# Conversion of w_k split between TensorE and GpSimd, VectorE's start in a written order, and fewer, larger loads

## The chip, the cores and the metric

The kernel runs on one core of a Trainium2 chip. The metric is the device time of one execution in microseconds (us); the median of several runs is compared.

## The reference

Three stages follow each other, for 8 batches of 576 positions. Linear attention with an RMS norm gives `x`; a gated two-layer network with a one-position shift turns it into a second `x`; a causal attention of four experts (two chosen per position) gives the output. The first two stages, in which all of the change lies:

```python
kv  = np.einsum('bhsd,bhse->bhde', k, v)             # 8 heads of 64
out = np.einsum('bhsd,bhde->bhse', q, kv)
x   = out / np.sqrt(np.mean(out * out, -1, keepdims=True) + 1e-6) * g_norm
...
xk = mu_k * x + (1.0 - mu_k) * x_prev                # x_prev: x one position earlier
xr = mu_r * x + (1.0 - mu_r) * x_prev
k  = np.maximum(xk @ w_k, 0.0)                       # 512 x 1024
v  = k * k @ w_v                                     # 1024 x 512
r  = 1.0 / (1.0 + np.exp(-(xr @ w_r)))               # 512 x 512
return r * v
```

## The kernel before

Every large product runs as three fp32r matmuls: an operand is split into a high and a low half, and high by high, high by low and low by high are added in PSUM (`mm3`, lines 75 to 79). A batch's 576 positions are cut into two halves (h) of 288.

Phase A goes through the batches. Its **front** (`Front`) forms kv from five chunks of k and v (`chunk`, L294), multiplies by q (`heads`, L311), forms mean squares (`means`, L323), takes their inverse root on VectorE in a chain of steps that each need the one before (`rsqrt`, L329 to L338), spreads it over the partitions with TensorE (`spread`, L345) and scales x (`scaled`, L351). A **mix** (`mix`) makes the inputs `xr` or `xk` of one half: for each of four 128-row pieces ScalarE scales the shifted x, VectorE adds the other part (`xm`, L402), ScalarE rounds it to the high half `mixh`, VectorE subtracts for the low half `mixl` (L397). An **r group** is 12 matmuls with w_r and a sigmoid, a **k group** 12 matmuls with w_k, a Relu on ScalarE and a square on GpSimd (`ksq`). Batch 0 has 8 r groups and 16 k groups.

The weights w_r, w_k and w_v come as 64-bit floats. `converted` turns a 128 by 512 chunk of w_r (chunks 0 to 3) or w_k (4 to 11) into halves: ScalarE takes the absolute value of the upper word, VectorE builds an fp32 number `t` from it in three steps (L213, L215, L217), ScalarE rounds it to the high half, VectorE makes the part that the lower word adds in two steps (L204, L206). TensorE then adds `t`, minus the high half and minus that part in PSUM (L249 to L251), and ScalarE writes the sum out as the low half. There are three buffers for `t` (`cvt`). `value_blocks` converts w_v likewise during batches 1 to 6, with an addition on GpSimd (L468) in the place of TensorE's sum, one buffer `vraw` for the loaded words, and one step per `run(vals)`.

**What sets the order.** The tile framework's scheduler orders each engine's instructions by its own estimate of time. Instructions issued through `vec`, `act` and `ten` (class `InOrder`) while their `on` is set keep their written order among themselves; others are put between them. Before, all three are on until the r groups of batch 0's first half are written, and then off. Loads and stores go through the queues of SyncE and ScalarE; in the built program each transfer takes the next of eight semaphores in rotation, and is issued only when the semaphore's previous transfer has landed.

At the end of the conversions for w_r VectorE has the means' chain of batch 0, two mixes for w_r, then the mixes for w_k and the conversions that are left; TensorE can start r groups when the first mix is there, and k groups when chunks 4 to 7 and the first mix for w_k are there.

Of the kernel before, what the change touches and what calls it, by code (L numbers as in the profile page):

```python
# [25 lines left out]
def tile_kernel(ctx: ExitStack, tc: tile.TileContext, qT, k, v, g2, mu_k, mu_r, w_r, w_k, w_v, w_qk, w_vg, w_o, out):  # L26
    nc = tc.nc
    P = 128
    B, S, DM = k.shape
# [23 lines left out]
    g_sb = const.tile([P, 1], F32, name="g_sb")  # L53
    muk = const.tile([P, KD], F32, name="muk")
    mur = const.tile([P, KD], F32, name="mur")
    nuk = const.tile([P, KD], F32, name="nuk")
    nur = const.tile([P, KD], F32, name="nur")
# [124 lines left out]
    def phase_a():  # L182
        W["vb"] = ExitStack()
        vb = W["vb"].enter_context(tc.tile_pool(name="vb", bufs=1, side="right", reuse_waits="tile"))
        with ExitStack():
# [71 lines left out]
            def load_kv(i, eng=nc.sync):  # L257
                b, c = divmod(i, NF)
                if b < B and i not in kvt:
# [4 lines left out]
                    kvt[i] = (kt, vt)  # L264

            def load_q(i, eng=nc.sync):
                b, c = divmod(i, 4)
                if b < B and i not in qts:
                    qt = fr.tile([P, 2, HS], F32, name="qt", bufs=4)
                    eng.dma_start(qt, qT[b, c])  # L270
                    qts[i] = qt
# [3 lines left out]
            class Front:  # L275
# [10 lines left out]
                def chunk(self, c):  # L286
                    t0, n = FH[c]
                    kt, vt = kvt[self.b * NF + c]
                    for a in range(NP):

                        for r in range(2):
                            hd = 2 * (2 * (a // 2) + r) + a % 2
                            hd = slice(hd * D, (hd + 1) * D)
                            ten.matmul(self.kw[r * D:(r + 1) * D, a, :], kt[:n, hd], vt[:n, hd],  # L294
                                       start=(c == 0 and a == 0), stop=(c == NF - 1), skip_group_check=True)
                    load_kv((self.b + 1) * NF + c)
# [7 lines left out]
                def heads(self, h, a):  # L304
                    i = 4 * self.b + 2 * h + a
                    qt = qts[i]
                    po = pf.tile([P, 2, 512], F32, name="po", bufs=2)
                    for c in range(2):
                        for r in range(2):
                            rs = slice(r * D, (r + 1) * D)  # L310
                            ten.matmul(po[c * D:(c + 1) * D, r, :HS], self.kv[rs, 2 * a + c, :], qt[rs, c, :], start=True, stop=True, skip_group_check=True)  # L311
                    load_q(i + 4)
# [123 lines left out]
            def value_blocks():  # L436
# [23 lines left out]
                def value(n):  # L460
                    nonlocal raw
                    t = fr.tile([P, CW], F32, name="cvt", bufs=3)
# [46 lines left out]
            for i in range(4):  # L509
                load_q(i)  # L510
            for i in range(KD, len(wts)):
                wload(i, nc.sync)
            for nu, mu in ((nuk, muk), (nur, mur)):
                vec.tensor_scalar(nu, mu, -1.0, 1.0, op0=ALU.mult, op1=ALU.add)
# [52 lines left out]
            for e in (vec, act, ten):  # L567
                e.on = False
# [41 lines left out]
            for b in range(1, B):  # L610
# [9 lines left out]
                for n, (g, h, m) in enumerate(groups):  # L620
# [10 lines left out]
                    run(f, vals)  # L631
                    if n < 2 * KD:
# [488 lines left out]
```

## Time and profile before

| | |
|---|---|
| median of 3 runs | 1000.81 us (999.16 to 1003.89) |
| profiled execution, its time | 996.78 us |
| its span, first to last instruction | 995.0 us |
| TensorE matmul busy | 955.1 us (96%) |
| VectorE / ScalarE / GpSimd busy | 643.1 / 538.8 / 414.4 us |
| mean granted TensorE clock | 0.991 of full |

The profile of one execution gives, for each instruction, its engine, line, output and inputs, start and length, the idle time of its engine just before, and what ended that idle time. A line of 67 is that of the recording helper, whatever the operation. Matmuls and VectorE instructions overlap at their ends, so the distance between two starts can be shorter than the length of the first. Phase A fills about the first 430 us, the second product (with w_v) follows until about 615 us, then the expert attention.

### The profile page before, as it was taken

How to read it: one execution, taken by the hardware profiler on the slowest of the kernel's cores; microseconds unless marked ns; L12 is line 12 of the kernel's file. 1: busy time of each engine (PE TensorE's matmuls, PEld its weight loads, DVE VectorE, ACT ScalarE, POOL GpSimd, SP SyncE). 2: the span in 40 equal slices, each digit the busy share in tenths (PEclk: the TensorE clock that was granted, in tenths of full speed). 3: DMA queues.
4: the chain of work that ended last, by engine and by line, in shares of the span. 5: the costliest groups of instructions: out<-in, count | busy, mean ns of one | idle time of the engine just before them, and what ended most of it. 6: DMA issues, size and time to landing. Idle time of an engine off the chain costs nothing.

```text
span 995.0 us, 21152 instructions
## 1 busy us (share of the span) xinstructions
PE 955.1 (96%) x7936; PEld 871.4 (88%) x7936; DVE 643.1 (65%) x1532; ACT 538.8 (54%) x1326; POOL 414.4 (42%) x510
## 2 busy tenths in 40 slices
PE   5599999999999999999999999999999999999998
PEld 3478898999999989999899999888989888888986
DVE  4874694856585945549888884566555565656562
ACT  5583756565665756445544442546364546455544
POOL 0013052424251513465878886436162534335231
PEclk9799999999999999999999999999999999999999
DMA  9652737263726313858566652002020202020102
GB/s 328 225 182 80 225 100 224 76 232 112 234 103 214 105 67 98 291 180 250 177 235 196 210 161 100 27 23 84 14 96 2 96 7 90 27 70 27 49 13 84
DMA packets 82742, 127.22 MB, mean 128 GB/s; under 512 B 7632, under 2 KB 58320, under 8 KB 82640
## 3 DMA queue, kind: packets, MB, share of 16 engines
q1 hardware_dynamic: 65744, 104.11, 31.6%
q10 hardware_dynamic: 16896, 21.76, 7.0%
q8 instruction: 63, 1.03, 0.4%
q14 instruction: 39, 0.32, 0.1%
HBM read 78.66 MB, written 47.19 MB: 126 GB/s over the span
## 4 chain that ended last, share of the span: by engine, by line
PE 74%; DVE 8%; DMA 6%; ACT 6%; POOL 3%; issue 2%; SPq 0%; ACTq 0%; DVEq 0%; POOLq 0%
PE acc L77 15%; PE acc L78 14%; PE acc L79 14%; PE qa L671 6%; PE qd L671 4%; PE acc L671 4%; PE pt L940 3%; PE acc L967 3%; DMA x2in<-x2d 3%; PE s L891 3%; ACT pr L903 2%; POOL x2l L777 2%; PE acc L294 2%; POOL pr L920 1%; DMA vt<-in_v 1%
## 5 line engine op out<-in xcount | busy, mean ns | idle before, releaser
L431 POOL TENSOR_TENSOR ksq<-rl 128x288 f32<-128x288 f32 x128 | 97.3, 765 | 162.2 <-ACT rl L429 157.9
L77 PE MATMUL acc<-mixh,wkh 128*128 128x288 f32 x512 | 152.6, 298 | 0.0
L78 PE MATMUL acc<-mixl,wkh 128*128 128x288 f32 x512 | 152.1, 297 | 0.0
L79 PE MATMUL acc<-mixh,wkl 128*128 128x288 f32 x512 | 151.0, 295 | 0.0
L903 ACT ACTIVATE pr<-pr,nm 128x256 f32<-128x256 f32 (+4 forms) x144 | 83.2, 580 | 65.0 <-DVE nm L857 64.8
L920 POOL TENSOR_SCALAR pr<-pr,rc,wg 128x512 f32<-128x512 f32 (+3 forms) x128 | 76.7, 612 | 99.6 <-DVE wg L850 60.8
L77 PEld LDWEIGHTS acc<-mixh,wkh 128*128 128x128 f32 x512 | 96.0, 187 | 1.9 <-issue 1.1
L79 PEld LDWEIGHTS acc<-mixh,wkl 128*128 128x128 f32 x512 | 96.4, 188 | 0.7 <-issue 0.4
L78 PEld LDWEIGHTS acc<-mixl,wkh 128*128 128x128 f32 x512 | 96.1, 188 | 0.9
L683 POOL TENSOR_TENSOR sgv<-ct,sgv 128x288 f32<-128x288 f32 x64 | 81.3, 1294 | 36.6 <-DVE ct L681 36.0
L429 ACT ACTIVATE rl<-acc 128x288 f32<-128x288 f32 x128 | 51.9, 407 | 76.9 <-PE acc L79 64.5
L397 DVE TENSOR_TENSOR mixl<-xm,mixh 128x288 fp32r<-128x288 f32 x120 | 59.8, 530 | 50.1 <-ACT mixh L403 49.6
L857 DVE CUSTOM_DVE_ANT_0 pr<-s,mask 128x256 f32<-128x256 f32 (+4 forms) x144 | 66.9, 482 | 18.8 <-PE pt L940 11.8
L77 PE MATMUL acc<-mixh,wrh 128*128 128x288 f32 x240 | 73.9, 308 | 0.5 <-ACT sg L67 0.5
L77 PE MATMUL acc<-x2h,wqh 128*128 128x320 f32 (+1 forms) x240 | 74.3, 310 | 0.0
L79 PE MATMUL acc<-mixh,wrl 128*128 128x288 f32 x240 | 72.1, 300 | 0.0
L78 PE MATMUL acc<-mixl,wrh 128*128 128x288 f32 x240 | 72.0, 300 | 0.0
L79 PE MATMUL acc<-x2h,wql 128*128 128x320 f32 (+1 forms) x240 | 71.1, 296 | 0.0
L78 PE MATMUL acc<-x2l,wqh 128*128 128x320 f32 (+1 forms) x240 | 70.9, 295 | 0.0
L73 DVE TENSOR_TENSOR kk<-tv,kk 128x1152 fp32r<-128x1152 f32 x32 | 58.7, 1852 | 8.4 <-ACT kk L72 8.4
L940 PE MATMUL pt<-ident,pr 128*128 128x128 f32 x400 | 62.6, 276 | 1.1 <-ACT pt L949 0.5
L72 ACT ACTIVATE kk<-tv 128x1152 fp32r<-128x1152 f32 x32 | 37.3, 1167 | 38.5 <-POOL tv L160 15.6
(236 smaller groups left out, 2788.0 us busy)
## 6 DMA issues: line engine op xcount, KB each, us to landing
kkd<-ksq SPq DMA_DIRECT2D x128, 144.0 KB, 1.8
kin<-kkd SPq DMA_DIRECT2D x32, 576.0 KB, 4.9
qt<-in_qT SPq DMA_DIRECT2D x32, 288.0 KB, 4.8
sgv<-sgd SPq DMA_DIRECT2D x16, 576.0 KB, 3.8
x2d<-sgv SPq DMA_DIRECT2D x16, 576.0 KB, 3.2
sgd<-sg ACTq DMA_DIRECT2D x56, 144.0 KB, 3.5
out<-ob SPq DMA_DIRECT2D x28, 288.0 KB, 2.1
kt<-in_k SPq DMA_DIRECT2D x24, 256.0 KB, 4.6
```

What stands on the lines that cost most here:

```text
L73: vec.tensor_sub(lo, src, hi.bitcast(F32))
L77: ten.matmul(ps, wh(i), xh(i), start=(i == 0), stop=False)
L78: ten.matmul(ps, wh(i), xl(i), start=False, stop=False)
L79: ten.matmul(ps, wl(i), xh(i), start=False, stop=(i == n - 1))
L397: vec.tensor_sub(xl[:, p, :], xs[p], xh[:, p, :].bitcast(F32))
L431: nc.gpsimd.tensor_mul(sq, rl, rl)
L671: nc.tensor.matmul(q[:, :HS], a[:, i, ms_], c[:, i, :], start=(start and i == 0 and n == 0), stop=(stop and i == KH - 1 and n == 2), skip_ ...
L683: nc.gpsimd.tensor_mul(g, c, g)
L857: nc.vector.tensor_tensor_reduce(out=pr[:R, k0:k0 + kn], in0=s[:R, :kn], in1=mk, scale=1.0, scalar=lo, op0=ALU.add, op1=ALU.min, accum_out ...
L903: nc.scalar.activation(pr[:, :L], pr[:, :L], AF.Exp, bias=nm, scale=-1.0, accum_out=sms[b, p, j][:, e2:e2 + 1])
L920: nc.gpsimd.tensor_scalar(pr[:, :L], pr[:, :L], rc[:, r:r + 1], wg, op0=ALU.mult, op1=ALU.mult)
L940: nc.tensor.transpose(pt[:, (i - i0) * P:(i - i0 + 1) * P], pr[:, k1 - P:k1], ident)
```

## The change

1. `vec` stays on longer, until the first mix for w_k is written, so that VectorE's steps of the means, the mixes for w_r, the conversions 4 to 7 and that mix keep their written order. Steps of chunks 8 to 11 are still placed by the scheduler.
2. Chunks 6 to 11 (`LATE = 6`) get their low half otherwise: VectorE's lower-word step writes `vd`, of which there is one buffer, GpSimd adds it to `t`, ScalarE rounds the high half from the sum, VectorE subtracts for the low half. The three matmul steps and ScalarE's copy of these six chunks are gone.
3. k and v of a chunk come in one transfer; q comes in two transfers per batch (two buffers) and not in four; `g_norm`, `mu_k` and `mu_r` come in one transfer on ScalarE's queue and not in three on SyncE's, and the two `1 - mu` steps are one.
4. `value` yields twice before it starts, and every eighth group runs one step more of `vals`.

```diff
@@ weights of phase A @@
+    pars = const.tile([P, 1 + 2 * KD], F32, name="pars")
+    nus = const.tile([P, 2 * KD], F32, name="nus")
+    g_sb, muk, mur = pars[:, :1], pars[:, 1:1 + KD], pars[:, 1 + KD:]
+    nuk, nur = nus[:, :KD], nus[:, KD:]
...
-            wts, raws = [], []
+            wts, raws, LATE = [], [], 6
@@ converted @@
                 next(words)
                 yield
                 next(words)
-                act.activation(h, t, AF.Copy)
-                yield
-                for _ in low_word(lo, hi, t.bitcast(I32), l, -2.0 ** -52):
-                    pass
-                yield
-                acc = acc_tile()
-                ten.matmul(acc, ident, t, start=True, stop=False)
-                ten.matmul(acc, idn, h, start=False, stop=False)
-                ten.matmul(acc, idn, l, start=False, stop=True)
-                act.activation(l, acc, AF.Copy)
+                if i < LATE:
...
+                else:
+                    yield
+                    d = conv.tile([P, CW], F32, name="vd")
+                    for _ in low_word(lo, hi, t.bitcast(I32), d, 2.0 ** -52):
+                        pass
+                    nc.gpsimd.tensor_add(t, t, d)
+                    yield
+                    act.activation(h, t, AF.Copy)
+                    vec.tensor_sub(l, t, h.bitcast(F32))
                 yield
@@ loads @@
-                    kt, vt = [fr.tile([P, DM], F32, name=name, bufs=5) for name in ("kt", "vt")]
-                    nc.sync.dma_start(kt[:n], k[b, t0:t0 + n, :])
-                    eng.dma_start(vt[:n], v[b, t0:t0 + n, :])
+                    t = kvt[i] = fr.tile([P, 2, DM], F32, name="kvt", bufs=5)
+                    nc.sync.dma_start(t[:n].rearrange("p u d -> p (u d)"), kv[b, t0:t0 + n, :])
...
-                    qt = fr.tile([P, 2, HS], F32, name="qt", bufs=4)
-                    eng.dma_start(qt, qT[b, c])
+                    qts[i] = fr.tile([P, 2, 2, HS], F32, name="qt", bufs=2)
+                    nc.sync.dma_start(qts[i], qT[b, h])
...
-                    load_q(i + 4)
+                    if a == 1:
+                        load_q(2 * self.b + h + 2)
@@ value @@
                     nonlocal raw
+                    yield
+                    yield
                     t = fr.tile([P, CW], F32, name="cvt", bufs=3)
@@ start of phase A @@
-            for u, src in ((g_sb, g2), (muk, mu_k), (mur, mu_r)):
-                nc.sync.dma_start(u, src)
             for i in range(KD):
                 wload(i, (act, nc.sync)[i % 2])
+                if i == 1:
+                    act.dma_start(pars, par)
...
             for e in (vec, act, ten):
                 e.on = True
+            vec.tensor_scalar(nus, pars[:, 1:], -1.0, 1.0, op0=ALU.mult, op1=ALU.add)
...
             for m in range(KD):
                 r_group(0, 0, m)
-            for e in (vec, act, ten):
-                e.on = False
+            act.on = ten.on = False
...
                 run(mk)
                 if m < 3:
                     f1.chunk(m + 2)
+            vec.on = False
             f1.state()
@@ later batches @@
                     run(f, vals)
+                    if n % 8 == 7:
+                        run(vals)
```

VectorE, at the means' chain of batch 0 (`ms`, `nt`, `y` are its tiles; `cvt_531` and `cvt_558` are chunks 5 and 6 of w_k). Before:

```order
L67 TENSOR_SCALAR y_374<-nt_375 128x144
L213 TENSOR_SCALAR cvt_531<-cvt_531 128x512
L67 TENSOR_TENSOR nt_375<-y_374 128x144
L215 TENSOR_SCALAR cvt_531<-cvt_531 128x512
L213 TENSOR_SCALAR cvt_558<-cvt_558 128x512
L67 TENSOR_TENSOR nt_375<-nt_375,ms_373 128x144
L217 SCALAR_TENSOR_TENSOR cvt_531<-raw_160,cvt_531 128x512
L215 TENSOR_SCALAR cvt_558<-cvt_558 128x512
L67 SCALAR_TENSOR_TENSOR y_374<-nt_375,y_374 128x144
```

Now:

```order
L66 TENSOR_SCALAR ms_339<-acc_322 128x144
L66 TENSOR_SCALAR nt_341<-ms_339 128x144
L66 TENSOR_SCALAR y_340<-nt_341 128x144
L66 TENSOR_TENSOR nt_341<-y_340 128x144
L66 TENSOR_TENSOR nt_341<-nt_341,ms_339 128x144
L66 SCALAR_TENSOR_TENSOR y_340<-nt_341,y_340 128x144
```

The ten steps of these two chunks that stood between the chain's steps stand behind the mixes for w_r now.

VectorE, behind the last low half for w_r (`mixl`). Before, the first mix for w_k (`xm_671`, `mixl_670`) begins even ahead of it (`mixl_444`):

```order
L402 SCALAR_TENSOR_TENSOR xm_671<-xT_307,muk_86,xm_671 128x288
L67 TENSOR_TENSOR mixl_444<-xm_456,mixh_443 128x288
L402 SCALAR_TENSOR_TENSOR xm_673<-xT_307,muk_86,xm_673 128x288
L397 TENSOR_TENSOR mixl_670<-xm_671,mixh_669 128x288
L402 SCALAR_TENSOR_TENSOR xm_689<-xT_307,muk_86,xm_689 128x288
L397 TENSOR_TENSOR mixl_670<-xm_673,mixh_669 128x288
```

Now twelve steps of chunks 4 to 6 come first, then these: the last of chunk 6 (`cvt_524`), four of chunk 8 (`cvt_590`), the new subtraction of chunk 6, and chunk 7 (`cvt_553`); 26 rows stand between the last `mixl` for w_r and the first `xm` for w_k:

```order
L66 SCALAR_TENSOR_TENSOR vd_558<-raw_143 128x512
L212 TENSOR_SCALAR cvt_590<-cvt_590 128x512
L214 TENSOR_SCALAR cvt_590<-cvt_590 128x512
L216 SCALAR_TENSOR_TENSOR cvt_590<-raw_147,cvt_590 128x512
L203 TENSOR_SCALAR raw_147<-cvt_590 128x512
L66 TENSOR_TENSOR wkl_115<-cvt_524,wkh_114 128x512
L66 TENSOR_SCALAR cvt_553<-cvt_553 128x512 x2
```

The conversions that stood in the chain, and those of chunks 6 to 9, have moved ahead of the first mix for w_k, and the second mix stands between steps of chunks 10 and 11.

TensorE, at the first k group. Before, behind the last r group:

```order
L249 MATMUL acc<-cvt,ident 128x512
L250 MATMUL acc<-wkh,idn 128x512
L251 MATMUL acc<-wkl,idn 128x512
L294 MATMUL acc<-vt,kt 64x64 x29
L77 MATMUL acc<-mixh,wkh 128x288
L78 MATMUL acc<-mixl,wkh 128x288
L79 MATMUL acc<-mixh,wkl 128x288
```

Now:

```order
L300 MATMUL acc<-kvt 64x64 x32
L316 MATMUL po<-qt,kv 64x288 x16
L76 MATMUL acc<-mixh,wkh 128x288 x4
L77 MATMUL acc<-mixl,wkh 128x288
L78 MATMUL acc<-mixh,wkl 128x288
```

All of the next batch's `heads` stand ahead of the k groups now, and four k groups are open at once, piece by piece of the mix; the next four are ordered likewise, and the means of batch 1 stand behind those eight.

## Rows read from the trace of the kernel before

**Rows 1.** Busy time by stretch: start:end us, length, busy per engine, PEclk, DMA share, GB/s

```profile
0.00:47.78 47.78, 26.43 (x224) 18.05 (x225) 32.73 (x82) 25.81 (x49) 1.85 (x17) 0.86 0.81 281
47.78:100.18 52.40, 52.40 (x432) 43.52 (x433) 29.64 (x68) 32.63 (x74) 10.60 (x16) 1.00 0.41 131
100.00:430.00 330.00, 326.26 (x2992) 306.15 (x2991) 213.20 (x428) 200.47 (x480) 114.82 (x139) 0.99 0.49 161
```

**Rows 2.** Timeline of TensorE: start us, us, line, what [idle before, releaser]

```profile
33.67 1.13 PE L67 MATMUL po<-rb,selb 32*128 32x144 f32 x8 [8.59 <-DVE rb L67]
...
47.78 0.40 PE L77 MATMUL acc<-mixh,wrh 128*128 128x288 f32 x1 [0.49 <-ACT sg L67]
...
84.23 1.19 PE L323 MATMUL acc<-sq,sels 128*32 128x144 f32 x32
...
100.18 0.29 PE L77 MATMUL acc<-mixh,wrh 128*128 128x288 f32 x1
```

**Rows 3.** Timeline of VectorE: the means' chain of the first batch, same columns

```profile
25.13 0.31 DVE L67 TENSOR_SCALAR ms<-acc 128x144 f32<-128x144 f32 x1 [6.73 <-PE acc L67]
...
26.01 0.43 DVE L213 TENSOR_SCALAR cvt<-cvt 128x512 f32<-128x512 f32 x1
26.35 0.30 DVE L67 TENSOR_TENSOR nt<-y 128x144 f32<-128x144 f32 x1
...
30.93 0.69 DVE L206 SCALAR_TENSOR_TENSOR wkl<-raw 128x512 fp32r<-128x512 uint32 x1
31.53 0.30 DVE L67 SCALAR_TENSOR_TENSOR y<-nt,y 128x144 f32<-128x144 f32 x1
31.86 0.31 DVE L67 TENSOR_TENSOR nt<-y 128x144 f32<-128x144 f32 x1
...
33.16 0.37 DVE L67 SCALAR_TENSOR_TENSOR rb<-rb,lom,y 128x144 fp32r<-128x144 f32 x1
```

**Rows 4.** Timeline of VectorE: the end of the mixes for w_r

```profile
45.79 0.52 DVE L402 SCALAR_TENSOR_TENSOR xm<-xT,muk,xm 128x288 f32<-128x288 f32 x1
46.22 0.45 DVE L67 TENSOR_TENSOR mixl<-xm,mixh 128x288 fp32r<-128x288 f32 x1
```

**Rows 5.** Chain that ended last, in order of time: start us, us, what

```profile
49.38 0.86 PE acc L249 x2
50.24 0.23 PE acc L250
50.47 0.14 PE acc L78
...
50.74 0.24 PE acc L251
```

**Rows 6.** Timeline of VectorE: first and last step of w_r's fourth chunk

```profile
15.60 0.88 DVE L67 TENSOR_SCALAR cvt<-cvt 128x512 f32<-128x512 f32 x2
...
17.71 0.69 DVE L67 SCALAR_TENSOR_TENSOR wrl<-raw 128x512 fp32r<-128x512 uint32 x1
```

**Rows 7.** Timelines of VectorE and GpSimd: an addition for w_v beside the means' chain

```profile
125.05 1.35 DVE L333 TENSOR_TENSOR nt<-y 128x144 f32<-128x144 f32 x1
...
124.94 1.29 POOL L468 TENSOR_TENSOR cvt<-cvt,vd 128x512 f32<-128x512 f32 x1 [7.31 <-DVE vd L206]
```

**Rows 8.** Timelines of VectorE and ScalarE: the start

```profile
6.91 0.17 DVE L514 TENSOR_SCALAR nur<-mur 128x4 f32<-128x4 f32 x1 [1.34 <-DMA mur<-in_mu_r]
...
5.22 0.66 ACT L67 ACTIVATE cvt<-raw 128x512 f32<-128x512 f32 x1 [2.44 <-DMA raw<-in_w_r]
```

**Rows 9.** Timelines of TensorE (two rows) and ScalarE (one): waits in the later batches

```profile
131.34 0.67 PE L345 MATMUL po<-rb,selb 32*128 32x144 f32 x8 [1.45 <-DVE rb L338]
...
164.41 0.71 PE L311 MATMUL po<-qt,kv 64*64 64x288 f32 x8 [1.87 <-ACT xT L315]
...
163.16 0.65 ACT L314 ACTIVATE sq<-po 128x576 f32<-128x576 f32 x1 [4.42 <-DMA vraw<-in_w_v]
```

**Rows 10.** Busy time by stretch: behind TensorE's wait at 164 us

```profile
164.00:170.00 6.00, 5.59 (x35) 4.15 (x36) 2.08 (x5) 5.60 (x14) 0.10 (x1) 0.72 0.96 284
```

More of the change, by code (lines that the diff above doesn't have):

```diff
@@ L25, in tile_kernel @@
 @with_exitstack
-def tile_kernel(ctx: ExitStack, tc: tile.TileContext, qT, k, v, g2, mu_k, mu_r, w_r, w_k, w_v, w_qk, w_vg, w_o, out):
+def tile_kernel(ctx: ExitStack, tc: tile.TileContext, qT, kv, par, w_r, w_k, w_v, w_qk, w_vg, w_o, out):
     nc = tc.nc
     P = 128
-    B, S, DM = k.shape
+    B, S, DM = kv.shape[0], kv.shape[1], kv.shape[2] // 2
     H = 8
@@ L242, in converted @@
                 next(words)
-                act.activation(h, t, AF.Copy)
-                yield
-                for _ in low_word(lo, hi, t.bitcast(I32), l, -2.0 ** -52):
-                    pass
-                yield
-                acc = acc_tile()
-                ten.matmul(acc, ident, t, start=True, stop=False)
-                ten.matmul(acc, idn, h, start=False, stop=False)
-                ten.matmul(acc, idn, l, start=False, stop=True)
-                act.activation(l, acc, AF.Copy)
+                if i < LATE:
+                    act.activation(h, t, AF.Copy)
+                    yield
+                    for _ in low_word(lo, hi, t.bitcast(I32), l, -2.0 ** -52):
+                        pass
+                    yield
+                    acc = acc_tile()
+                    ten.matmul(acc, ident, t, start=True, stop=False)
+                    ten.matmul(acc, idn, h, start=False, stop=False)
+                    ten.matmul(acc, idn, l, start=False, stop=True)
+                    act.activation(l, acc, AF.Copy)
+                else:
+                    yield
+                    d = conv.tile([P, CW], F32, name="vd")
+                    for _ in low_word(lo, hi, t.bitcast(I32), d, 2.0 ** -52):
+                        pass
+                    nc.gpsimd.tensor_add(t, t, d)
+                    yield
+                    act.activation(h, t, AF.Copy)
+                    vec.tensor_sub(l, t, h.bitcast(F32))
@@ L253, in converted, with load_kv @@
                 yield
             kvt, qts = {}, {}
-            def load_kv(i, eng=nc.sync):
+            def load_kv(i):
                 b, c = divmod(i, NF)
-                if b < B and i not in kvt:
+                if b < B:
                     t0, n = FH[c]
-                    kt, vt = [fr.tile([P, DM], F32, name=name, bufs=5) for name in ("kt", "vt")]
-                    nc.sync.dma_start(kt[:n], k[b, t0:t0 + n, :])
-                    eng.dma_start(vt[:n], v[b, t0:t0 + n, :])
-                    kvt[i] = (kt, vt)
@@ L266, in load_q @@
-            def load_q(i, eng=nc.sync):
-                b, c = divmod(i, 4)
-                if b < B and i not in qts:
-                    qt = fr.tile([P, 2, HS], F32, name="qt", bufs=4)
-                    eng.dma_start(qt, qT[b, c])
-                    qts[i] = qt
+                    t = kvt[i] = fr.tile([P, 2, DM], F32, name="kvt", bufs=5)
+                    nc.sync.dma_start(t[:n].rearrange("p u d -> p (u d)"), kv[b, t0:t0 + n, :])
+            def load_q(i):
+                b, h = divmod(i, 2)
+                if b < B:
+                    qts[i] = fr.tile([P, 2, 2, HS], F32, name="qt", bufs=2)
+                    nc.sync.dma_start(qts[i], qT[b, h])
@@ L310, in heads @@
                             rs = slice(r * D, (r + 1) * D)
-                            ten.matmul(po[c * D:(c + 1) * D, r, :HS], self.kv[rs, 2 * a + c, :], qt[rs, c, :], start=True, stop=True, skip_group_check=True)
-                    load_q(i + 4)
+                            ten.matmul(po[c * D:(c + 1) * D, r, :HS], self.kv[rs, 2 * a + c, :], qt[rs, a, c, :], start=True, stop=True, skip_group_check=True)
+                    if a == 1:
+                        load_q(2 * self.b + h + 2)
                     sq = self.sq[h, a] = fr.tile([P, 2, HS], F32, name="sq", bufs=4)
@@ L461, in value @@
                     nonlocal raw
+                    yield
+                    yield
                     t = fr.tile([P, CW], F32, name="cvt", bufs=3)
@@ L501, in phase_a @@
                     wts.append((wkh[:, i, c:c + CW], wkl[:, i, c:c + CW], w_k, i * P, c))
-            for u, src in ((g_sb, g2), (muk, mu_k), (mur, mu_r)):
-                nc.sync.dma_start(u, src)
             for i in range(KD):
                 wload(i, (act, nc.sync)[i % 2])
+                if i == 1:
+                    act.dma_start(pars, par)
             for i in range(NF):
                 load_kv(i)
-            for i in range(4):
+            for i in range(2):
                 load_q(i)
```

24 lines of the change are left out of this document (7 added, 17 removed).

## The prediction

> **What bounds the kernel now.** I read the busy time by stretch first, then TensorE's timeline, then VectorE's at TensorE's waits. From 100 to 430 us TensorE is busy for 326.26 of 330 us; from 47.78 to 100.18 all the time, in the first 47.78 us for 26.43 only [rows 1]. So work that TensorE loses, or a start that comes sooner, counts in full as long as nothing else becomes late. The start is VectorE's: TensorE waits 8.59 us for the inverse root of the means, and the first r group of the second half starts at 47.78; the means of batch 1 come at 84.23, batch 1's first r group at 100.18 [rows 2]. The sum is made on this profiled execution, 996.78 us; the three runs have a median of 1000.81, and I carry the difference over to that.
>
> **The start.** VectorE waits 1.34 us for mur until 6.91, while ScalarE's first absolute value is done at 5.22 + 0.66 = 5.88 [rows 8]. With one parameter load the first step can come up to 1.0 us sooner. Against that, the first tile of k and v is now issued beside w_r's first chunk, which can land later. Between 1.0 us gained and 0.5 lost I take 0.5 gained.
>
> **The means' chain.** It runs from 25.13 to 33.16 + 0.37 = 33.53, 8.40 us, with ten w_k steps in it; steps that follow each other alone are 0.33 to 0.35 us apart (31.53 to 31.86) [rows 3]. Three first steps take 0.88 us (25.13 to 26.01), nine at 0.345 make 3.10, the cast and the last step 0.64: 4.62. Gain 3.78 us. This has one answer, since VectorE does nothing else there.
>
> **The mixes for w_r.** Three steps of chunk 4 leave the stretch between the chain and the first mix: two SCALAR_TENSOR_TENSOR of 0.60 each (30.93 to 31.53) and one TENSOR_SCALAR of 0.34 (26.01 to 26.35) [rows 3], 1.54 together; the xm for w_k ahead of the last mixl leaves too, 0.43 us (45.79 to 46.22) [rows 4]. I count 1.9. So far 0.5 + 3.8 + 1.9 = 6.2 us: the r group of 47.78 starts at 41.6, and VectorE is done with the mixes for w_r at 46.22 + 0.45 - 6.2 = 40.5.
>
> **Six chunks less on TensorE.** One costs 0.86 + 0.23 + 0.24 = 1.33 us (rows of L249, L250, L251) [rows 5]; six make 8.0 us, all in the stretch where TensorE is the bound. ScalarE loses six copies and gains nothing. With these two gains alone batch 1 would begin at 100.18 - 6.2 - 8.0 = 86.0.
>
> **What is late next.** Everything that left the start, and six new subtractions, now stands on VectorE ahead of or between the mixes for w_k. From 40.5 it has: three steps left of chunk 4, 1.8 us (two thirds of a chunk); seven chunks, at 17.71 + 0.60 - 15.60 = 2.7 us in series [rows 6], or 2.2 where two chunks interleave (three steps of 0.34, two of 0.60 [rows 3]): 5.4 for chunks 5 and 6 in series and 5 x 2.45 = 12.3 for the others; six subtractions, for which no row of that size exists before: between 0.45 (a mixl of 288 columns [rows 4]) and 0.80 (0.45 scaled to 512), taken as 0.60, the step of 512 columns in [rows 3], 3.6; eight xm and eight mixl at 0.43, 6.9. Sum 30.0 us: 70.5.
>
> The six additions on GpSimd are the unknown price. The same operation for w_v takes 1.29 us, and the VectorE step that runs beside it takes 1.35 [rows 7] in place of the 0.30 of the same step at 26.35 [rows 3]: 1.05 us lost each, 6.3 in all, if VectorE always has a step to lose, as here it has. Bounds: 0 and 6 x 1.29 = 7.7. I take 6.3, the row that is nearest, and VectorE ends at 76.8; its last mixl is one subtraction earlier, 76.2.
>
> The Trainium skill ("SBUF — State Buffer", "SBUF: two separate sides") says that VectorE and GpSimd share a port pair as an exclusive lock, held for the whole instruction, so that a VectorE step with two SBUF inputs waits until GpSimd's is over. It speaks against moving these sums to GpSimd beside a saturated VectorE; the row of 1.35 agrees with it. By it each addition would cost up to its whole length, 7.7 us in place of 6.3, and batch 1 would begin 1.4 us later.
>
> In TensorE's new order the eight k groups of the first four column blocks come before the means of batch 1, four open at a time, so that behind the last mixl only eight matmuls of 0.14 [rows 5] are left: 76.2 + 1.1 = 77.3. From the means to batch 1's first r group I keep 100.18 - 84.23 = 15.95 [rows 2]: 93.3. TensorE then waits some 7 us in pieces between about 58 and 76. Behind one wait of 1.87 us at 164 its granted clock averaged 0.72 over 6 us [rows 9, 10], a loss of 1.7. So there is a price of the clock here, between 0 and twice that; I take 1.0. Batch 1 begins at 94.3, a gain of 5.9 where 14.2 were taken out.
>
> **The larger loads and w_v's spacing.** The loads lie beside a busy TensorE from 48 us on, so fewer of them are worth nothing by themselves. But a rotation of eight is passed more slowly. At 158.7 us ScalarE has a store to issue whose semaphore's last user is the vraw load eight transfers earlier; it stands for 4.42 us until that load lands, its next work starts at 163.16, and TensorE waits 1.87 us, with the clock loss of 1.7 behind it [rows 9, 10]. With five loads per batch in place of ten between them, and the load placed otherwise, the eighth transfer comes several groups later. I count 3.6 us. The other wait, 1.45 us at 131.34 for rb [rows 9], is in a chain with w_v steps in it; they still stand there, only later in the chain, so I count 0 to 1.45 and take 0. Two more yields per `value` and three more steps per batch move no work: cover is TensorE's own 326 of 330 us; without that cover a late half of w_v would stop the second product, but 150 steps at 27 a batch end as early as 134 at 24 (5.6 batches). Bounds for the whole item: 0 and 5.1. The scheduler also orders the expert attention's first batches a little differently: 1.5 us either way, taken as 0.
>
> **Sum.** 6.2 + 8.0 - (94.3 - 86.0) = 5.9, and 3.6: 9.5 us off 996.78, 987.3 by the profiled execution; from the median 1000.81, **991.3 us**.
>
> **Rivals.**
> - *GpSimd costs VectorE nothing* and the clock stays up. VectorE's last mixl is then at 69.9, TensorE goes through at 69.9 + 1.1 + 15.95 = 87.0, the gain is 13.2 + 3.6, with rb's wait 1.45 more: some 18 us, 983. For it: the steps of one input may run beside an addition. Against it: the row of 1.35.
> - *The wait eats the gain.* The additions cost their full length (1.4 more), the clock loses 3.4 in place of 1.0, and the store's wait comes back at another transfer: 9.5 - 1.4 - 2.4 - 3.6 = 2.1 us, 998.7, no change that can be measured. For it: every number of this stretch sits on one saturated engine, and any transfer of vraw's size can hold the rotation.
> - *Slower.* A late chunk goes around: VectorE's vd, GpSimd's sum, ScalarE's rounding, VectorE's subtraction, with one vd buffer and three cvt buffers, and ScalarE stands behind the four heads of batch 1 there. If a chunk has to wait for that circle, it costs 0.69 (30.93), 1.29, 0.66 (as ScalarE's step at 5.22) and 0.60, about 3.2 us [rows 3, 7, 8], in place of the 1.05 for each of six: 13 us more. To be slower by 5 us the last mixl must come after 76.2 + 9.5 + 5 = 91. The steps of two other chunks between fill the circle in the new order, and that speaks against it: then about 1004.
> - *The order is not held*: not a case by itself, since the new program shows the chain without w_k steps; the unpinned steps of chunks 8 to 11 ahead of the mix are in the sum.
>
> **Chances.** Forecast as summed, 986 to 995: 0.55. GpSimd free or nearly so: 0.17. Wait eats the gain: 0.22. Slower: 0.06. A measurement of this kernel tells 0.5%, 5 us, from no change. A part of the forecast's own spread lies above 995.8: faster 0.71, within 0.5% 0.24, slower 0.05. The range reaches from the full gain of the first rival to most of the second: 983 to 999.
>
> **What would show it.** The means' chain at 4.6 us; TensorE's first r group of the second half near 41.6; no L249 for six chunks; VectorE without idle time from there to about 76, with steps beside the additions over 1 us; TensorE's new waits for mixl between 58 and 77; batch 1's first r group near 94; no wait at the third batch's heads. I am wrong if TensorE has no waits there (VectorE lighter than summed), if batch 1 begins later than 98, or if the gain of the first 100 us is lost again after it.

## The result

| | before | after |
|---|---|---|
| median of 4 runs each, same chip | 1002.18 us (999.16 to 1003.89) | 991.33 us (990.46 to 991.88) |
| ratio | | 0.9906, 95% interval 0.9883 to 0.9929 |
| span of the profiled execution | 995.0 us | 989.9 us |

The time came out where it was predicted, and 1% faster is more than the measurement is uncertain. The forecast started from the 1000.81 us of three runs; with the fourth the median of before is 1002.18, so the gain is 10.85 us where 9.5 was forecast. But the two profiled executions lie only 5.1 us apart, half of what the medians do, and the terms of the sum did not come out as written. Six marks show where the time went. They are read from the traces: **ms** is VectorE's first step of the means' chain, **r** TensorE's first r group of batch 0's second half, **b1** batch 1's first r group, **middle** from there to the first matmul of the second product, **second** that product up to the start of its last matmul, **rest** what follows to the end of the span (these two to within 0.1 us). The second row is a second profile of the unchanged kernel (experiment 1).

| kernel | ms | r | b1 | middle | second | rest | span |
|---|---|---|---|---|---|---|---|
| before | 25.13 | 47.78 | 100.18 | 321.7 | 191.8 | 381.3 | 995.0 |
| before, second profile | 25.24 | 47.89 | 100.27 | 326.0 | 192.1 | 381.4 | 999.8 |
| after | 27.08 | 44.67 | 97.82 | 315.3 | 190.5 | 386.3 | 989.9 |

So b1 comes 2.4 us sooner (5.9 forecast), the middle is 6.4 or 10.7 us shorter (3.6 forecast), and the rest is 5 us longer (0 forecast).

**The start and VectorE's chain, after.** TensorE's timeline, to hold against [rows 2]; columns are start, length, line and what, and the idle time before with its releaser:

```profile
31.83 1.13 PE L66 MATMUL po<-rb,selb 32*128 32x144 f32 x8 [4.80 <-DVE rb L66]
...
44.67 0.40 PE L76 MATMUL acc<-mixh,wrh 128*128 128x288 f32 x1 [0.58 <-ACT sg L66]
...
64.76 1.33 PE L76 MATMUL acc<-mixh,wkh 128*128 128x288 f32 x4 [2.78 <-ACT mixh L409]
...
81.87 1.19 PE L329 MATMUL acc<-sq,sels 128*32 128x144 f32 x32
...
97.82 0.29 PE L76 MATMUL acc<-mixh,wrh 128*128 128x288 f32 x1
```

VectorE's timeline, to hold against [rows 3, 8]: the wait for the parameters, and the chain:

```profile
7.74 0.17 DVE L66 TENSOR_SCALAR nus<-pars 128x8 f32<-128x8 f32 x1 [5.20 <-DMA pars<-in_par]
...
27.08 0.31 DVE L66 TENSOR_SCALAR ms<-acc 128x144 f32<-128x144 f32 x1 [6.92 <-PE acc L66]
...
31.31 0.37 DVE L66 SCALAR_TENSOR_TENSOR rb<-rb,lom,y 128x144 fp32r<-128x144 f32 x1
```

The chain lasts 31.31 + 0.37 - 27.08 = 4.60 us (before 8.40), and TensorE's wait for it falls from 8.59 to 4.80. But it begins 1.95 us later than before.

**The stretch with the additions, after.** Busy time by stretch, as [rows 1] (length; then busy PE, PEld, DVE, ACT, POOL; granted clock, DMA share, GB/s):

```profile
44.67:97.82 53.15, 47.00 (x408) 41.63 (x409) 44.82 (x86) 31.50 (x71) 21.16 (x22) 0.94 0.40 129
100.00:430.00 330.00, 329.39 (x3039) 311.03 (x3034) 210.85 (x431) 202.53 (x482) 120.90 (x148) 1.00 0.51 166
```

TensorE's sums are gone and the stretch is as long as before: 53.15 us with 6.15 idle, where it was 52.40 with none. From 100 to 430 us it is idle for 0.61 us (before 3.74). What TensorE waited for from 44.67 to 97.82 us (total us, times, longest); `xT` and `kv` are ScalarE's copies in the front of batch 1:

```profile
PE acc L76 <- ACT mixh L409: 2.8, 1, 2.8
PE po L316 <- ACT xT L321: 2.1, 2, 1.2
...
PE po L316 <- ACT kv L305: 0.5, 1, 0.5
PE acc L77 <- DVE mixl L66: 0.2, 1, 0.2
```

The waits of 0.83, 1.25 and 2.78 us at 59 to 65 us stand close together, and there the granted clock falls:

```profile
63.00:71.00 8.00, 6.24 (x28) 6.12 (x29) 7.63 (x16) 6.25 (x14) 2.25 (x2) 0.57 0.44 150
```

That is a loss of 0.43 x 8 = 3.4 us.

### The profile page after: what moved, and what is told of

It reads as the page before. It is cut to its first block, busy times and chain, and to the rows that moved or that the text cites. A ratio compares the mean times of both kernels' runs of the same rounds, so it can differ in the third digit from the quotient of the medians.

```text
span 989.9 us, 20990 instructions
## 1 busy us (share of the span) xinstructions
PE 949.4 (96%) x7912; PEld 870.1 (88%) x7912; DVE 651.5 (66%) x1537; ACT 536.3 (54%) x1320; POOL 427.0 (43%) x516
## 4 chain that ended last, share of the span: by engine, by line
PE 76%; DVE 7%; ACT 7%; DMA 5%; POOL 3%; issue 2%; ACTq 0%; DVEq 0%; POOLq 0%
PE acc L76 16%; PE acc L77 15%; PE acc L78 15%; PE qa L680 6%; PE qd L680 4%; PE acc L680 4%; DMA x2in<-x2d 3%; PE acc L976 3%; PE pt L949 3%; PE s L900 2%; ACT pr L912 2%; POOL x2l L786 2%; PE acc L300 2%; POOL pr L929 1%; PE po L316 1%
## 5 line engine op out<-in xcount | busy, mean ns | idle before, releaser
L437 POOL TENSOR_TENSOR ksq<-rl 128x288 f32<-128x288 f32 x128 | 99.5, 783 | 148.2 <-ACT rl L435 142.7
L77 PE MATMUL acc<-mixl,wkh 128*128 128x288 f32 x512 | 154.3, 302 | 0.2 <-DVE mixl L66 0.2
L435 ACT ACTIVATE rl<-acc 128x288 f32<-128x288 f32 x128 | 51.6, 405 | 71.5 <-PE acc L78 52.7
L408 DVE SCALAR_TENSOR_TENSOR xm<-xT,pars,xm 128x288 f32<-128x288 f32 x116 | 69.0, 624 | 5.1 <-ACT xm L400 5.0
L400 ACT ACTIVATE xm<-xT,nus 128x288 f32<-128x288 f32 x120 | 61.0, 532 | 18.8 <-DVE mixl L403 9.2
```

Of the source, the lines that this page charges most:

```text
L77: ten.matmul(ps, wh(i), xl(i), start=False, stop=False)
L400: act.activation(xs[p], xT[:, p, h * HS:(h + 1) * HS], AF.Copy, scale=nu[:, p:p + 1])
L408: vec.scalar_tensor_tensor(xs[p], xT[:, p, cols(h)], mu[:, p:p + 1], xs[p], op0=ALU.mult, op1=ALU.add)
L437: nc.gpsimd.tensor_mul(sq, rl, rl)
```

## The experiments

All marks, in the same columns; time and ratio are against the kernel before on the same chip. Experiments 1 to 4, experiments 5, 6, 8 and 9, and experiments 7 and 10 to 12 are three sets, each with its own runs of before (medians 1000.50, 1000.78 and 1004.13 us); across the sets the ratios are to be compared, not the times.

| kernel | time | ratio (95%) | ms | r | b1 | middle | second | rest |
|---|---|---|---|---|---|---|---|---|
| 1 before again | 1000.62 | 0.9998 (0.9981, 1.0015) | 25.24 | 47.89 | 100.27 | 326.0 | 192.1 | 381.4 |
| 2 sums on TensorE | 989.25 | 0.9885 (0.9856, 0.9914) | 25.46 | 43.05 | 97.32 | 315.2 | 191.1 | 382.1 |
| 3 old spacing | 990.69 | 0.9903 (0.9874, 0.9933) | 27.09 | 44.70 | 97.83 | 315.3 | 190.5 | 386.6 |
| 4 one column | 985.43 | 0.9847 (0.9813, 0.9881) | 26.73 | 44.32 | 92.61 | 315.2 | 190.5 | 385.7 |
| 5 only order | 1000.00 | 0.9990 (0.9972, 1.0007) | 26.06 | 43.66 | 96.80 | 324.5 | 192.5 | 383.9 |
| 6 only loads | 995.60 | 0.9958 (0.9936, 0.9981) | 25.18 | 47.87 | 100.18 | 315.3 | 193.1 | 384.9 |
| 7 only spacing | 995.64 | 0.9920 (0.9895, 0.9945) | 25.25 | 47.89 | 100.29 | 318.8 | 191.8 | 381.8 |
| 8 start's loads | 990.70 | 0.9898 (0.9877, 0.9919) | 23.39 | 41.19 | 95.56 | 315.3 | 190.7 | 387.9 |
| 9 four sums | 987.88 | 0.9868 (0.9847, 0.9890) | 23.70 | 41.36 | 95.08 | 315.2 | 191.0 | 384.0 |
| 10 five sums | 986.31 | 0.9833 (0.9796, 0.9869) | 26.13 | 43.54 | 96.04 | 315.2 | 191.2 | 381.8 |
| 11 one sum | 983.11 | 0.9799 (0.9769, 0.9830) | 24.31 | 41.90 | 93.71 | 315.3 | 190.7 | 381.3 |
| 12 stores on SyncE | 994.18 | 0.9910 (0.9878, 0.9943) | 26.06 | 48.70 | 101.10 | 316.1 | 195.3 | 381.9 |

**1. The kernel before, once more** (no edit).

> The kernel before, unchanged, profiled a second time. Its first profiled execution took 996.78 us, while its four timed runs took 999.16 to 1003.89. Theory A: the expert attention costs the changed kernel 5 us (386 us from the last matmul of the second product to the end, against 381.1 in the first profile of before). Then a second profile of before shows 381 us there again, and its extra 3 to 7 us lie in the first 620 us. Theory B: before's first profile was a lucky execution, and the attention differs from one execution to the next by that much. Then the second profile shows 384 to 387 us there without any change of the kernel.

The rest is 381.4 again: theory A. Before's own spread sits in the middle, which was 4.3 us longer this time; its timed runs in this set went from 996.29 to 1003.36. The same load stops ScalarE as in [rows 9], for longer; ScalarE's timeline of this second profile:

```profile
165.13 0.65 ACT L314 ACTIVATE sq<-po 128x576 f32<-128x576 f32 x1 [4.85 <-DMA vraw<-in_w_v]
```

**2. Sums back on TensorE.**

```diff
-            wts, raws, LATE = [], [], 6
+            wts, raws, LATE = [], [], 12
```

> The changed kernel with LATE = 12: all low halves of w_k's chunks by TensorE and ScalarE as before, no addition on GpSimd; order of VectorE, loads and spacing stay changed. Theory A (the additions and the subtractions cost VectorE what the six sums save TensorE): VectorE's stretch from the last mixl for w_r to the last mixl of the first k mix falls from 35.9 by 6.3 + 3.6 to about 26 us; TensorE's waits there, 6.2 us, and about 1 us of clock go, 8.0 us of sums come back; batch 1's first r group moves from 97.8 to about 98.6, and the time by +1, to 992 to 993. Theory B (part 2 of the change carries the gain): TensorE was the bound before and is again, batch 1's first r group comes 5 to 8 us later, at 103 to 106, and the time is 996 to 999.

From r to b1, TensorE busy all the time:

```profile
43.05:97.32 54.27, 54.27 (x433) 44.09 (x433) 35.16 (x80) 34.27 (x77) 10.92 (x16) 1.00 0.40 126
```

It takes 54.27 us against 53.15, so the six additions bring 1.1 us there, not 5 to 8: theory A. Even this 1.1 us is no more than the order of the same work is worth: with all sums on TensorE, no idle time and the clock at 1.00, the stretch took 52.40 us before, 53.14 in experiment 5 and 54.27 here. VectorE's stretch fell to 27.5 us (about 26 expected). The time lies below both theories' ranges and even slightly below the changed kernel's (0.9885 against 0.9906): ms came 1.6 us sooner with the same loads, and the rest was 4.2 us shorter, which experiment 10 looks into.

**3. Old spacing of w_v's steps.** The changed kernel without the two `yield`s and the `n % 8` step.

```diff
                 def value(n):
                     nonlocal raw
-                    yield
-                    yield
...
-                    if n % 8 == 7:
-                        run(vals)
```

> The changed kernel with w_v's steps as close as before: no two yields at the start of a value, no extra step in every eighth group. Theory A (the spacing removes the waits of the middle): between batch 1's first r group and the first matmul of the second product the distance goes from 315.3 back to 318.9 to 321.8 us, with one TensorE wait of 1 to 2 us near 130 to 165 and a fall of the clock behind it; time 995 to 998. Theory B (the larger loads, which halve the transfers in the rotation of semaphores, remove them): the distance stays at 315 to 316.5 and the time within 1.5 us of the changed kernel.

Theory B: the middle stays at 315.3, and TensorE has no wait in it.

**4. The addition cut to one column.**

```diff
-                    nc.gpsimd.tensor_add(t, t, d)
+                    nc.gpsimd.tensor_add(t[:, :1], t[:, :1], d[:, :1])
```

> The changed kernel with GpSimd's addition for chunks 6 to 11 cut to one column of 512, so most of the lower word of these six chunks of w_k is left out; all waits stay. Theory A (the addition itself stops VectorE for about its length): VectorE's stretch from the last mixl for w_r to the last mixl of the first k mix falls from 35.9 to 29 to 30.5 us (6 x 0.9 to 1.05 less), no VectorE step of one input there is over 0.8 us, TensorE's waits of 6.2 us fall to 1 us or less, batch 1's first r group comes 5 to 6.5 us sooner, at 91 to 93, time 985 to 987. Theory B (the chain vd, sum, rounding, subtraction is what is slow, not the shared access): the steps stay short with the length of the addition gone, but the stretch falls by under 2 us and batch 1 begins at 96 or later.

Theory A, a little smaller. VectorE's stretch, from the last mixl for w_r to the end of the last mixl for w_k of batch 0, falls from 35.9 to 30.95 us (43.03 to 73.98): 0.83 us for each addition. TensorE is idle for 3.47 us from r to b1 (after: 6.15; 1 or less was expected), and 2.8 of these are the waits for xT and kv, which stay although the additions are cut. Its granted clock there is 1.00 (after: 0.94), and b1 comes 5.2 us sooner, 4.9 of it from r on. The same VectorE steps, after and then here, with GpSimd's additions:

```profile
51.09 1.27 DVE L212 TENSOR_SCALAR cvt<-cvt 128x512 f32<-128x512 f32 x1 [0.48 <-ACT cvt L210]
...
57.67 0.68 DVE L216 SCALAR_TENSOR_TENSOR cvt<-raw,cvt 128x512 int32<-128x512 int32 x1
58.38 1.39 DVE L203 TENSOR_SCALAR raw<-cvt 128x512 int32<-128x512 int32 x1
...
50.80 1.28 POOL L258 TENSOR_TENSOR cvt<-cvt,vd 128x512 f32<-128x512 f32 x1 [48.08 <-DVE vd L66]
57.92 1.55 POOL L258 TENSOR_TENSOR cvt<-cvt,vd 128x512 f32<-128x512 f32 x1 [5.84 <-DVE vd L66]
```

```profile
50.73 0.43 DVE L212 TENSOR_SCALAR cvt<-cvt 128x512 f32<-128x512 f32 x1 [0.47 <-ACT cvt L210]
...
56.68 0.43 DVE L203 TENSOR_SCALAR raw<-cvt 128x512 int32<-128x512 int32 x1
...
56.94 0.21 POOL L258 TENSOR_TENSOR cvt<-cvt,vd 128x1 f32<-128x1 f32 x1 [6.32 <-ACT kv L305]
```

1.27 and 1.39 us become 0.43: the addition held them, though they have one input only. The step that was under way when the addition of 57.92 began kept its 0.68 us.

**5. Only VectorE's order, on the kernel before.**

```diff
-            for e in (vec, act, ten):
-                e.on = False
+            act.on = ten.on = False
...
+            vec.on = False
             f1.state()
```

> The kernel before with part 1 of the change alone: VectorE's order held up to the first k mix. Theory A: the means' chain falls from 8.4 to 4.6 us, the mixes follow 1.4 to 1.9 sooner, the first r group of the second half starts at 42.1 to 42.7 (before 47.8), batch 1 at 94.5 to 95; between batch 1 and the second product nothing is gained (321.7 and 326.0 us in the two profiles of before). In the expert attention the scheduler's order of ScalarE differs from before's and is that of the changed kernel, and the stage costs 385.5 to 386.6 us in place of 381.3; time 998 to 1001, no change. Theory B: the attention takes 381 to 382 whatever that order, and what the changed kernel loses there comes from another part; time 994 to 996.

From ms to r it takes 17.60 us (before 22.65, after 17.59), so part 1 brings 5.05 us there; b1 is 3.4 sooner. Both r (43.66) and b1 (96.80) came later than expected, 0.9 us of it ahead of ms. The middle stays long (324.5), and the rest is 2.6 longer than before's. No change in time, as theory A has it, though the rest, 383.9, lies between the two theories.

**6. Only the loads, on the kernel before.** Part 3 of the change alone; the core:

```diff
-                    nc.sync.dma_start(kt[:n], k[b, t0:t0 + n, :])
-                    eng.dma_start(vt[:n], v[b, t0:t0 + n, :])
+                    t = kvt[i] = fr.tile([P, 2, DM], F32, name="kvt", bufs=5)
+                    nc.sync.dma_start(t[:n].rearrange("p u d -> p (u d)"), kv[b, t0:t0 + n, :])
```

> The kernel before with part 3 of the change alone: larger and fewer loads. Theory A (the loads remove the waits of the middle): from batch 1's first r group to the first matmul of the second product 315 to 316 us (before 321.7 and 326.0); the first step of the means at 25.5 to 27.1 us (before 25.1); the attention in the slower order, 385.5 to 386.6; together 1000.5 - 8.6 + 1.2 + 4.7, 996 to 999. Theory B (the order of VectorE or w_v's spacing removes them): the middle stays at 321 to 326, and the time is 1004 to 1007.

Theory A: the middle is 315.3. But ms came at 25.18, as in before, and not at 25.5 to 27.1. ScalarE's waits on transfers from 100 to 420 us (total us, times, longest), before and then here:

```profile
ACT sq L314 <- DMA vraw<-in_w_v: 4.4, 1, 4.4
...
ACT sg L420 <- DMA kt<-in_k: 2.2, 1, 2.2
ACT sq L314 <- DMA vt<-in_v: 2.0, 2, 1.2
```

```profile
ACT sq L320 <- DMA sgd<-sg: 1.1, 1, 1.1
ACT sg L426 <- DMA sgd<-sg: 1.0, 1, 1.0
```

No wait for a load of k, v or w_v is left.

**7. Only the spacing, on the kernel before.** The lines that experiment 3 takes out, put into the kernel before.

> The kernel before with part 4 of the change alone: w_v's steps further apart. Theory A (the middle's waits come from the number of transfers, and the spacing does nothing, as the changed kernel without it showed): the middle, from batch 1's first r group to the second product, stays at 320 to 327 us with a wait of ScalarE on a load behind a store, the attention (whose order is before's) at 381.3, time 998 to 1003, no change. Theory B (either part alone would do): the middle falls to 315 to 317, time 991 to 995.

Neither theory whole: 318.8, some 3 to 7 us below before's two profiles. The time, 0.8% below its set's before, is faster by more than the interval. ScalarE still waits 8.3 us for kt and vt, about as long as in before (8.6 for vraw, kt and vt), but TensorE waits for 2.58 us only (3.74) and its clock stays at 1.00: a wait of ScalarE costs as much of it as reaches TensorE. The spacing helps where the many loads stand and adds nothing to the larger ones.

**8. The start's loads in a held order.** `syn` is SyncE recorded as `vec` is.

```diff
+            syn.on = act.on = True
+            syn.dma_start(pars, par)
             for i in range(KD):
-                wload(i, (act, nc.sync)[i % 2])
-                if i == 1:
-                    act.dma_start(pars, par)
+                wload(i, (act, syn)[i % 2])
             for i in range(NF):
                 load_kv(i)
+            syn.on = act.on = False
```

> The changed kernel with the loads of the start in a held order: the parameters first on SyncE's queue, then w_r's chunks, then the tiles of k and v behind them. Theory A (the start is late because a tile of k and v is issued ahead of w_r's chunk and the parameters stand behind another load): VectorE's first step for w_r at 6 to 6.9 us in place of 7.8, the first step of the means at 24.3 to 25.4 in place of 27.08, the first r group of the second half 1.7 to 2.7 sooner, and batch 1 at 95.1 to 96.5, time 988.5 to 989.8; the attention stays at 385.5 to 386.6. Theory B (the start depends on the bytes that are under way, not on their order): the first step at 7.2 or later, time 990.5 to 992.

The start follows theory A and more: VectorE's first step at 5.22, 2.6 us sooner, and ms 3.7; the other 1 us is mostly a pair of TensorE's matmuls, short here and long in the changed kernel (see the account of the start).

```profile
5.22 0.89 DVE L66 TENSOR_SCALAR cvt<-cvt 128x512 f32<-128x512 f32 x2 [1.30 <-ACT cvt L66]
```

Of this b1 keeps 2.3 us: from r to b1 it takes 54.37 us, with TensorE idle for 6.29 and its granted clock at 0.91. The time, 990.70, is in theory B's range, though the start is theory A's: the rest took 387.9, 1.6 more than after, and ate most of what was left.

**9. Four sums, with the start of 8.** `LATE = 8` in experiment 8's kernel.

> The kernel of e8 with LATE = 8: four of w_k's chunks by GpSimd in place of six; the scheduler's order of the attention comes out as that of before. Theory A (with six additions VectorE stops TensorE, with none TensorE is the bound, so fewer is better than both): from the first r group of the second half to batch 1's first r group 49.5 to 51.5 us (53.15 with six, 54.27 with none), batch 1 at 91.5 to 94, the middle 315.2, the attention 381 to 382.2; time 981 to 984.5. Theory B (each addition stops TensorE as long as it saves): that stretch stays at 53 to 54.5, time 985 to 987.

Theory A fell: from r to b1 53.72 us, and the rest was 384.0 although ScalarE's and VectorE's order there was before's (TensorE's was that of experiment 2, which took 382.1). The time, 987.88, is just above what theory B gave.

**10. Five sums.** `LATE = 7` in the changed kernel.

> The changed kernel with LATE = 7: five chunks by GpSimd in place of six. With this number the scheduler writes the expert attention in exactly before's order on TensorE, VectorE and ScalarE. Theory A (the 5 us that the changed kernel loses in the attention come from the other order of its first batches): the stage takes 381 to 382 us in place of 386.3, TensorE waits at most 1.5 us at a time in its first 20 us and its granted clock stays at 1.00 there; with batch 1 at 97 to 98.5 the time is 985.5 to 988. Theory B (they come from how the second product ends or from one execution to the next): 384 to 387, time 989 to 992.

Theory A: the rest is 381.8. The rows of the attention's first 20 us, from the end of the second product on: TensorE's wait and its busy time in 20 us (columns as above). After:

```profile
618.51 0.41 PE L76 MATMUL acc<-x2h,wqh 128*128 128x320 f32 x1 [3.47 <-DVE vs L829]
...
603.60:623.60 20.00, 15.70 (x114) 14.96 (x113) 7.43 (x25) 7.75 (x22) 9.80 (x18) 0.91 0.29 89
```

Experiment 10:

```profile
618.89 0.39 PE L76 MATMUL acc<-wgh,x2h 128*128 128x260 f32 x1 [1.00 <-DVE ks L72]
...
602.40:622.40 20.00, 18.25 (x138) 16.38 (x137) 9.46 (x33) 7.75 (x22) 9.79 (x18) 1.00 0.28 89
```

Before:

```profile
630.55 0.39 PE L77 MATMUL acc<-wgh,x2h 128*128 128x260 f32 x1 [1.40 <-DVE ks L73]
...
613.70:633.70 20.00, 17.87 (x135) 15.99 (x133) 9.03 (x31) 7.75 (x22) 9.75 (x18) 1.00 0.29 90
```

In the changed kernel TensorE waits 3.47 us at one place, and its granted clock is 0.91 over the 20 us, a mean of its two levels (2.4 GHz is 1.00, 1.2 is half); with before's order the wait is 1.00 us and the clock full. In experiments 5 and 6, with the changed kernel's order of ScalarE, the longest wait there is 2.87 and 3.02 us, but the clock stays at 1.00: the order brings the wait, and only in some runs does the clock fall behind it. No code of this stage differs: the scheduler orders it, and a change 500 us ahead of it moves that order.

**11. One sum, with the start of 8.** `LATE = 11` in experiment 8's kernel.

> The kernel of e8 (loads of the start in a held order) with LATE = 11: one chunk by GpSimd; the attention again in before's order. Theory A (the gain lies in the loads and VectorE's order, and TensorE's sums cost no more than GpSimd's): first r group of the second half at 41.2 to 41.4, 52.5 to 54.5 us more to batch 1, so 93.7 to 95.8; middle 315.2, second product 191, attention 381.3 to 382.2; time 982.5 to 985.5, below every kernel that computes the whole. Theory B (five sums more on TensorE cost their full 1.33 us each against four on GpSimd, 54 + 4): batch 1 at 98 or later and a time of 987 to 989.

Theory A: 983.11 us, the fastest kernel of all by time and by ratio. From r to b1 it takes 51.81 us, less than the 52.5 expected, with TensorE never idle and its clock at 1.00 (r came at 41.90, 0.5 later than expected), and the attention is in before's order.

**12. The r groups' stores on SyncE, in the kernel before.**

```diff
-                (nc.sync if b == 0 else act).dma_start(sgd[b][:, m, h * HS:(h + 1) * HS], sg)
+                nc.sync.dma_start(sgd[b][:, m, h * HS:(h + 1) * HS], sg)
```

> The kernel before with one word changed: the stores of the r groups go through SyncE's queue in every batch, where before ScalarE issues them for batches 1 to 7. Loads stay as many and as small as before. Theory A (ScalarE stands behind its own store whose turn in the rotation waits for a load, and TensorE waits for ScalarE): ScalarE has no wait on a transfer over 1 us in the middle, TensorE's waits there fall from 3.7 us to under 1.5, the middle takes 315 to 318 us and the time 993 to 997 (plus up to 4 if the attention comes out in the slower order). Theory B (ten loads per batch cost by themselves, whoever issues the stores, or SyncE becomes the one that is late): the middle stays at 320 us or more.

Theory A: the middle is 316.1 with all small loads still there, TensorE has no wait in it from 101 to 418 us, and ScalarE waits for a transfer once, 0.2 us. What costs there is not the number of loads as such, but that ScalarE, which TensorE waits for, stands behind a store of its own. One reserve: the edit also moves some steps of ScalarE and VectorE in the scheduler's order, from about 106 us on, so this is the store together with what the scheduler makes of it. The second product took 195.3, 3.5 more. TensorE's waits for `ct` there are 4.6 us (before 3.9), and its granted clock averages 0.83 from 455 to 465 us, a loss of 1.7; what the store's new queue has to do with it was not followed further.

## Why the prediction was right, and where it was not

**The start: wrong in sign.** 0.5 gained with bounds +1.0 and -0.5; it was 1.95 lost. The failed step is the bound below: it priced the tile of k and v beside w_r's chunk, but not the parameters standing behind a 512 KB load. They landed 6.5 us after their issue, and VectorE's first step for w_r came at 7.82 in place of 6.99: 0.83. Issued first, in experiment 8, they landed after 3.0 us. The size of this loss is not fixed: in the six profiles with the same loads of the start (after and experiments 2, 3, 4, 6 and 10) they landed after 5.7 to 6.7 us, and the first step came at 6.96 (experiment 6, as in before) to 8.01. The other 1.1 us are on TensorE. The second chunk's two first matmuls took twice as long as before's; after, then before:

```profile
13.46 2.08 PE L66 MATMUL acc<-cvt,ident 128*128 128x512 f32 x2
14.54 1.33 PE L66 MATMUL acc<-wrh,idn 128*128 128x512 f32 x1
```

```profile
12.42 1.12 PE L67 MATMUL acc<-cvt,ident 128*128 128x512 f32 x2
13.41 0.50 PE L67 MATMUL acc<-wrh,idn 128*128 128x512 f32 x1
```

Experiment 5, whose loads are before's, has the long ones too (2.07 at 12.56); experiment 6, whose loads are the changed ones, has not (1.15 at 12.60). So this does not come from the loads, and what decides it stays open. With the same loads ms came at 25.18 to 27.09, so a term of 0.5 us could not have been read from one profile.

**The chain and the mixes: right.** 4.60 us where 4.62 was worked out, and from ms to r 5.06 us gained where 3.78 + 1.9 = 5.7 was.

**Six sums for six additions: right in the sum, in part by luck.** VectorE's stretch lasted 35.9 us (forecast 35.7), TensorE was idle for 6.15 us (forecast some 7), and from r to b1 it took 53.15 us where the sum gives 94.3 - 41.6 = 52.7. The rival in which GpSimd costs VectorE nothing fell; experiment 4 shows that its gain would have been about 5 us. Each addition costs 0.83 us net where 1.05 was taken. The Trainium skill ("SBUF — State Buffer", "SBUF: two separate sides") says that of two instructions of VectorE and GpSimd that both need the shared port pair, the one that starts first has it to its end and the other waits. The trace agrees: beside the addition of 57.92 the step of 58.38 was held, and the one begun at 57.67 was not; so an addition of 1.28 to 1.58 us need not cost its whole length.

The path was another, though. TensorE was to wait for mixl until VectorE's end; it waited 0.2 us for mixl, 2.8 us for one mixh of ScalarE, and 2.6 us for ScalarE's copies in batch 1's front, which the sum does not have and which stay, 2.8 us, in experiment 4. And the clock, taken as 1.0 us with 3.4 as its bound, cost 3.4. Less waiting for the mixes and more loss by the clock came out near the forecast together. That b1 was 2.4 us sooner and not 5.9 is the start (2.45 of 3.5) and, for the rest, the mixes and this stretch.

**The middle: right mechanism, mis-sized.** The term was 3.6 us, with 5.1 as its upper bound, and measured 6.4 and 10.7 against the two profiles of before. The store that waits for a load is the cause of the wait at 164 us, as said: experiments 6 and 12 remove it in different ways and reach 315.3 and 316.1. Two steps failed in size. The wait for rb, 1.45 us, was taken as 0 because w_v's steps stay in that chain, and it is gone too. And the bound counted the waits of one execution as all there was, though that execution, 996.78 us, was faster than the timed runs beside it. In the second profile TensorE was idle in the middle for 5.06 us (first 3.74, after 0.61), and the clock fell behind the wait for rb as well and for longer behind the other (columns as in [rows 1]):

```profile
130.00:137.00 7.00, 5.55 (x34) 5.31 (x34) 5.80 (x14) 2.83 (x8) 1.40 (x2) 0.76 0.54 163
...
165.00:175.00 10.00, 8.63 (x64) 6.46 (x68) 2.08 (x5) 7.61 (x17) 0.10 (x1) 0.66 0.73 209
```

That is 0.24 x 7 + 0.34 x 10 = 5.1 us of clock where the first profile lost 1.7 and the changed kernel none. Idle time and clock together make 4.8 of the 6.4 us and some 9.5 of the 10.7; the rest was not located. That the spacing was needed, as the heading of that item suggested, is not so (experiment 3).

**The attention: not forecast.** "1.5 us either way, taken as 0" was 5.0 lost. With before's order of ScalarE and VectorE in this stage it took 381.3 to 382.1 in seven profiles and 384.0 in experiment 9; with the changed kernel's order of ScalarE 383.9 to 387.9 in six (the changed kernel's own and experiments 3 to 6 and 8). Experiment 9 shows that the order is not all of it. The long wait and the clock of its first 20 us are the visible part, in TensorE's rows 17.87 - 15.70 = 2.2 us less work in these 20 us, and 1.4 to 1.8 us of clock (0.09 of 15.70 busy or of 20); the other 1 to 1.5 us were not located.

So 991.3 was met in part by luck: a start that lost 2.4 us against the sum and an attention that lost 5 were balanced by a middle that gave 3 to 7 more. Chain and mixes came out as worked out, the exchange in its sum, the middle by its mechanism, the start and the attention not. One of the prediction's own signs of being wrong came true: the gain of the first 100 us, 2.4 us, was lost again after them, in the attention; only the middle made up for it. Between the profiled executions the change is 5.1 us against the first profile of before and 9.9 against the second, between the medians 10.85; the last microsecond is not accounted for.

## What to carry to other kernels

Look first for the engine that everyone waits for and that also issues transfers: one word that moved its stores to another queue was worth 0.9% here (with the new order that the scheduler made of it), almost as much as the whole change. An addition handed to GpSimd beside a full VectorE is an exchange, not a gain: of 0, 1, 4, 5 and 6 additions, one gave the shortest stretch from r to b1 here (1 and 4 with the start of 8). Look at the stages behind as well, since a scheduler that re-orders them can lose half of what was won. Profile the old kernel twice before sizing a term from its waits.

## What the hardware showed that was not expected

- VectorE steps with a single SBUF input are held by a GpSimd addition as well: 1.27 and 1.39 us in place of 0.43.
- A load of nine words per partition took 5.7 to 6.7 us (six profiles) when issued 0.46 us behind a 512 KB load, and 3.0 to 3.3 (three) when issued first.
- In the first 15 us a pair of 512-column fp32 matmuls took 1.12 to 2.08 us, while the profile's granted clock stood at 1.00; in seven of the fourteen profiles the second chunk's pair still took over 1.5 us.
